# A gated scan layer re-cut into blocks of 1024 tokens, with one scan over two PSUM banks and the output projection six steps behind

## Chip, cores and metric

One core of a Trainium2 chip. The metric is the device time of one execution in microseconds (us), median of several runs. Engines are called as the profile calls them: PE (TensorE matmul), PEld (its weight loads), DVE (VectorE), ACT (ScalarE), POOL (GpSimd), SP (the queue that issues most transfers).

## The reference, cut to what matters

```
x: 8 sequences x 4224 tokens x 192      weight: 8 heads x 7 taps
w_in: 192 x 1024     A_log: 512     w_out: 512 x 192

x    = causal convolution of x along the tokens, softmax(weight) as taps, per head
proj = x @ w_in ;  val, gate = proj[..., :512], proj[..., 512:]
for t in range(S):                       # the scan, restarted in every sequence
    h = a * h + val[:, t] ;  ys[:, t] = h
out  = (silu(gate) * ys) @ w_out
```

The kernel computes in bf16 with fp32 sums and lays the 512 inner channels out as four groups (c = 0..3) of 128 partitions. All of its arithmetic is in SBUF and PSUM; the 33,792 tokens are walked in blocks.

## The kernel before

Blocks of 512 tokens, 66 of them. Per block: a convolution as matmuls against a banded matrix of taps (`tb`), eviction to bf16 (`xc`), then for each c a value projection (`pv`), a gate projection (`pg`), the scan on DVE, silu on ACT, the multiply `y`, and between them the output projection of the block before. Cut to what the argument touches:

```python
POOL_GATES = 2
    ps_c = ...tile_pool(name="ps_c", bufs=1, space=PSUM)     # pc: two banks
    ps_v = ...tile_pool(name="ps_v", bufs=2, space=PSUM)     # pv: one bank each
    ps_g = ...tile_pool(name="ps_g", bufs=2, space=PSUM)     # pg
    ps_o = ...tile_pool(name="ps_o", bufs=2, space=PSUM)     # po
    # ... taps: softmax, write 128 copies of the row to DRAM, read back shifted as tb ...
    # ... ab: decay table, 4 x 1024 fp32, built on DVE ...
    def cast(i, t):
        nc.gpsimd.tensor_copy(xbs[i % XB][:, :, 0:D], t)

    def scan(i, c, pv, prev):
        # ...
        nc.vector.tensor_tensor_scan(
            h, ab[:, c, a0 : a0 + N], pv,
            initial=prev[:, N - 1 : N] if prev is not None else 0.0,
            op0=Alu.mult, op1=Alu.add)

    def gate(i, c, pg, h):
        nc.scalar.activation(sg, pg, Act.Silu)
        eng = nc.gpsimd if c < POOL_GATES else nc.vector
        eng.tensor_mul(y, sg, h)

    for i in range(NS + 1):
        # load(i + 2); cast(i + 1)
        for c in range(NC):
            pv = proj(ps_v, "pv", xc, c)
            pg = proj(ps_g, "pg", xc, NC + c)
            hs[c] = scan(i, c, pv, hs[c])
            ys.append(gate(i, c, pg, hs[c]))
            outp(i - 1, ys_prev, c, ...)          # 4 matmuls, one per channel group
            # every second c: copy po to SBUF on ACT;  c == 1: conv(i + 1) and its eviction
        # store of block i - 1
```

## Time and profile before

| | before |
|---|---|
| time, median of three runs | 462.7 us (462.4 to 462.8) |
| profiled span | 460.6 us |
| busy: DVE / PE / ACT / POOL | 86% / 81% / 59% / 44% |
| period of 512 tokens | 6.43 us |
| first scan starts at | 31.5 us |

Busy shares are averages over the start, 66 like periods and the tail. The number that matters is the period, read from the starts of like instructions in order of time, and in it which wait ends last. The prediction shows these lines.

### The profile page before, as it was taken

What the parts mean: (1) busy time and instruction counts of PE and PEld (TensorE: products, weight loads), DVE (VectorE), ACT (ScalarE), POOL (GpSimd) and SP (SyncE); (2) the same over time, 40 slices, a digit from 0 to 9 for tenths busy, and PEclk for the clock granted to TensorE, in tenths of its full rate; (3) what the DMA queues carried; (4) which work ended last, traced back from release to release, by engine and by line L of the source; (5) the groups of instructions that cost most, each with busy time, mean ns of one, the idle gap of its engine ahead of it and who ended that gap; (6) DMA issues with size and microseconds to landing.
All of it is one profiled execution on the core that took longest, in us unless ns stands there. A gap on an engine that the chain in (4) does not pass through costs nothing.

```text
span 460.6 us, 11591 instructions
## 1 busy us (share of the span) xinstructions
PE 373.9 (81%) x4671; PEld 218.9 (48%) x4736; DVE 398.2 (86%) x415; ACT 271.9 (59%) x468; POOL 204.4 (44%) x205
## 2 busy tenths in 40 slices
PE   0048898888988898888988889888898888988884
PEld 0014555555554455554555545545454555555453
DVE  4259989999999999999999999999999999999995
ACT  1065666656665666656666566665666557665663
POOL 0114454445544455444554445544454445544442
PEclk9999999999999999999999999999999999999999
DMA  1901344433444334443444434444344433444323
GB/s 54 243 16 50 106 123 138 137 106 106 135 140 134 100 112 138 139 118 111 118 138 139 116 114 115 139 139 114 110 120 140 136 105 106 138 139 127 108 74 104
DMA packets 72469, 54.67 MB, mean 119 GB/s; under 512 B 4000, under 2 KB 72096, under 8 KB 72416
## 3 DMA queue, kind: packets, MB, share of 16 engines
q1 hardware_dynamic: 72128, 53.15, 40.1%
q10 hardware_dynamic: 288, 0.79, 0.7%
q8 instruction: 37, 0.61, 0.5%
q14 instruction: 16, 0.13, 0.1%
HBM read 27.44 MB, written 26.49 MB: 117 GB/s over the span
## 4 chain that ended last, share of the span: by engine, by line
DVE 51%; PE 38%; DMA 4%; issue 4%; ACT 1%; DVEq 1%; SPq 0%; ACTq 0%
DVE h L213 36%; PE pc L178 16%; DVE y L225 15%; PE po L230 9%; PE pv L203 7%; PE pg L203 7%; DMA wout<-in_moe_w_out_dram 2%; DMA win<-in_moe_w_in_dram 1%; DMA ws<-in_weight_dram 1%; DVEq L225 1%; DMA taps_scratch<-fz 1%; PE pc L187 1%; DVE fz L105 0%; SPq L130 0%; ACT xc L197 0%
## 5 line engine op out<-in xcount | busy, mean ns | idle before, releaser
L213 DVE TENSOR_TENSOR_SCAN h<-ab,h,pv 128x512 bf16<-128x512 f32 x260 | 324.5, 1269 | 22.4 <-PE pc L178 22.4
L225 POOL TENSOR_TENSOR y<-sg,h 128x512 bf16<-128x512 bf16 x132 | 152.5, 1155 | 226.2 <-DVE h L213 225.3
L222 ACT ACTIVATE sg<-pg 128x512 bf16<-128x512 f32 x264 | 157.6, 597 | 158.5 <-PE pg L203 158.5
L230 PE MATMUL po<-wout,y 128*128 128x192 bf16 x1056 | 141.3, 247 | 50.6 <-DVE y L225 50.6
L203 PE MATMUL pg<-xc,win 128*128 128x512 bf16 x528 | 157.7, 380 | 3.4
L230 PEld LDWEIGHTS <-y 128*128 128x128 bf16 x1056 | 95.9, 98 | 127.0 <-DVE y L225 65.6
L203 PE MATMUL pv<-xc,win 128*128 128x512 bf16 x463 | 144.6, 383 | 10.2 <-ACT xc L197 10.2
L203 PEld LDWEIGHTS <-win 128*128 128x128 bf16 x1056 | 95.3, 98 | 81.5 <-ACT win L150 8.7
L225 DVE TENSOR_TENSOR y<-sg,h 128x512 bf16<-128x512 bf16 x132 | 68.0, 515 | 14.2 <-DVE h L213 0.5
L197 ACT CAST xc<-pc 128x1024 bf16<-128x1024 f32 x66 | 66.8, 1012 | 0.1
L135 POOL CAST xb<-xraw 128x768 bf16<-128x768 f32 x66 | 54.6, 828 | 21.8 <-DMA xraw<-in_x_dram 19.9
L260 ACT COPY osb<-po 128x384 f32<-128x384 f32 x132 | 62.5, 474 | 2.1 <-issue 1.9
L178 PE MATMUL pc<-tb,xb 128*32 128x134 bf16 (+1 forms) x2112 | 46.6, 223 | 18.2 <-POOL xb L135 18.2
L178 PEld LDWEIGHTS <-xb 128*32 128x32 bf16 x2112 | 32.5, 95 | 28.8 <-POOL xb L135 18.2
L166 DVE TENSOR_SCALAR ab<-ab,av 128x1024 f32<-128x1024 f32 x4 | 2.7, 748 | 14.1 <-ACT av L162 14.1
L150 ACT CAST win<-win 128x2048 bf16<-128x2048 f32 x1 | 1.9, 1897 | 21.1 <-DMA win<-in_moe_w_in_dram 21.1
L187 PE MATMUL pc<-tb,xb 128*32 128x6 bf16 x512 | 13.1, 167 | 0.0
L187 PEld LDWEIGHTS <-xb 128*32 128x32 bf16 x512 | 10.6, 97 | 0.0
L213 DVE TENSOR_TENSOR_SCAN h<-ab,pv 128x512 bf16<-128x512 f32 x4 | 4.8, 1211 | 0.2
L164 DVE MEMSET ab<- 128x4096 f32 x1 | 3.5, 3472 | 0.8 <-issue 0.8
L95 DVE TENSOR_REDUCE wmax<-ws 128x8 f32<-128x56 f32 x1 | 0.2, 211 | 3.9 <-DMA ws<-in_weight_dram 3.9
L105 DVE MEMSET fz<- 128x2088 bf16 x1 | 1.8, 1798 | 0.4 <-issue 0.4
(16 smaller groups left out, 7.6 us busy)
## 6 DMA issues: line engine op xcount, KB each, us to landing
xraw<-in_x_dram SPq DMA_DIRECT2D x66, 384.0 KB, 3.9
out_dram<-osb SPq DMA_DIRECT2D x66, 384.0 KB
win<-in_moe_w_in_dram ACTq DMA_DIRECT2D x8, 96.0 KB
taps_scratch<-fz SPq DMA_DIRECT2D x1, 522.0 KB
wout<-in_moe_w_out_dram SPq DMA_DIRECT2D x1, 384.0 KB
tb<-taps_scratch SPq DMA_DIRECT2D x1, 268.0 KB
al<-in_moe_A_log_dram SPq DMA_DIRECT2D x4, 0.5 KB, 4.1
ws<-in_weight_dram SPq DMA_DIRECT2D x1, 28.0 KB
```

The costliest lines, as they stand in the source:

```text
L135: nc.gpsimd.tensor_copy(xbs[i % XB][:, :, 0:D], t)
L164: nc.vector.memset(ab, 1.0)
L166: nc.vector.tensor_scalar_mul(ab[:, c, :], ab[:, c, :], av[:, c : c + 1])
L178: nc.tensor.matmul(pc[q : q + 32, h // HG, b * P : b * P + w], xb[:, b, h * G : h * G + 32], tb[:, h, 0:w], start=(b == 0), stop=(b == NB ...
L187: nc.tensor.matmul(pc[q : q + 32, h // HG, 0:HALO], xp[:, NB - 1, h * G : h * G + 32], tb[:, h, P:W], start=False, stop=False, skip_group_ ...
L197: nc.scalar.copy(xc, pc)
L203: nc.tensor.matmul(ps, win[:, g, m * P : (m + 1) * P], xc[:, g, :], start=(g == 0), stop=(g == 1),)
L213: nc.vector.tensor_tensor_scan(h, ab[:, c, a0 : a0 + N], pv, initial=prev[:, N - 1 : N] if prev is not None else 0.0, op0=Alu.mult, op1=Al ...
L222: nc.scalar.activation(sg, pg, Act.Silu)
L225: eng.tensor_mul(y, sg, h)
L230: nc.tensor.matmul(po, ys[c][:, b * P : (b + 1) * P], wout[:, c, :], start=(c == 0 and b % 2 == 0), stop=(c == NC - 1), skip_group_check=True,
L260: nc.scalar.copy(osb[:, c - 1 : c + 1, :], po)
```

## The change

Intent: fewer and longer scans, less multiply work on DVE, no wait of PE for the last `y`, and a shorter start. Counted in banks, which here means places for a tile of up to 512 fp32 per partition, the kernel before takes eight of PSUM, two for each of its four pools. In the new one, two `pv` buffers of two banks and two banks for the convolution leave two of the same eight, which gate and output projection then share. The core of the diff:

```diff
-CAST = "pool"
-POOL_GATES = 2
+DVE_GATE = 1
+LAG = 6
...
-    ps_g = ctx.enter_context(tc.tile_pool(name="ps_g", bufs=2, space=bass.MemoryType.PSUM))
-    ps_o = ctx.enter_context(tc.tile_pool(name="ps_o", bufs=2, space=bass.MemoryType.PSUM))
+    ps_r = ctx.enter_context(tc.tile_pool(name="ps_r", bufs=2, space=bass.MemoryType.PSUM))
...
+    for h in range(H - 1):
+        nc.gpsimd.dma_start(                      # win straight to bf16, from POOL
+            win[C32 * (h % HG) : C32 * (h % HG) + C32, h // HG, :],
+            moe_w_in[h * G : h * G + C32, :],
+        )
...
-    nc.sync.dma_start(fa, fz.rearrange("p h f -> p (h f)"))
+    nc.scalar.dma_start(fa, fz.rearrange("p h f -> p (h f)"))
...
-            h, ab[:, c, a0 : a0 + N], pv,
+                h[:, lo:hi], av[:, c : c + 1].to_broadcast([P, hi - lo]), pv[:, lo:hi],
...
+    for s in range(NSTEP + LAG):                  # a step = one channel group of one block
+        i, c = divmod(s, NC)
+        if live:
+            # c == 0: load x three blocks ahead
+            scan(s)
+            if c == DVE_GATE + 1:
+                mul(nc.vector, s - 1)
+            gate(s, 0)
+        if s >= LAG:
+            outp(s - LAG)                         # 8 matmuls
+        if live:
+            if c % 2 == 0 and i + 1 < NS:
+                conv(2 * (i + 1) + c // 2)
+            val(s + 1, 0)
+            gate(s, 1)
+            val(s + 1, 1)
+            if c != DVE_GATE:
+                mul(nc.gpsimd, s)
+            else:
+                # cast x of two blocks ahead, on POOL
```

Also: six loads of x are issued at the start instead of two, the decay table is gone, and a block that holds the begin of a sequence gets its scan in two parts.

More of the change, by code (lines that the diff above doesn't have):

```diff
@@ L58 @@
     N = NB * P
+    N2 = 2 * N
     T = B * S
-    NS = T // N
+    NP = T // N
+    NS = T // N2
     BPB = S // P
@@ L63 @@
     HG = H // 2
-    assert NS * N == T and BPB * P == S and NC == 4 and G <= 32 and HG == 4
+    C32 = 32
+    assert NS * N2 == T and BPB * P == S and NC == 4 and G <= C32 and HG == 4
     W = P + HALO
-    XW = D + 8
     FL = P - 1
@@ L76 @@
     singles = ctx.enter_context(tc.tile_pool(name="singles", bufs=1))
-    xraw_pool = ctx.enter_context(tc.tile_pool(name="xraw", bufs=4))
-    xc_pool = ctx.enter_context(tc.tile_pool(name="xc", bufs=3))
+    xraw_pool = ctx.enter_context(tc.tile_pool(name="xraw", bufs=6))
+    xc_pool = ctx.enter_context(tc.tile_pool(name="xc", bufs=5))
     h_pool = ctx.enter_context(tc.tile_pool(name="hp", bufs=3))
@@ L84, with load @@
     ps_v = ctx.enter_context(tc.tile_pool(name="ps_v", bufs=2, space=bass.MemoryType.PSUM))
-    ps_g = ctx.enter_context(tc.tile_pool(name="ps_g", bufs=2, space=bass.MemoryType.PSUM))
-    ps_o = ctx.enter_context(tc.tile_pool(name="ps_o", bufs=2, space=bass.MemoryType.PSUM))
+    ps_r = ctx.enter_context(tc.tile_pool(name="ps_r", bufs=2, space=bass.MemoryType.PSUM))
+    XB = 4
+    raw = {}
+    def load(p):
+        t = xraw_pool.tile([P, NB, D], FP32, name="xraw")
+        nc.sync.dma_start(t, x4[p])
+        raw[p] = t
     FR = FL + W
@@ L93 @@
     )
+    load(0)
+    load(1)
+    win = singles.tile([P, 2, D2], BF16, name="win")
+    for h in range(H - 1):
[3 more added lines that the diff above has]
+        )
+    nc.gpsimd.dma_start(win[96 : 96 + G, 1, :], moe_w_in[(H - 1) * G : H * G, :])
+    nc.gpsimd.dma_start(win[96 + G : P, 1, :], moe_w_in[0 : C32 - G, :])
+    xbs = []
+    for j in range(XB):
+        xb = singles.tile([P, NB, H, C32], BF16, name=f"xb_{j}")
+        nc.gpsimd.memset(xb[:, :, :, G:C32], 0.0)
+        xbs.append(xb)
+    fz = singles.tile([P, H, FR], BF16, name="fz")
+    nc.vector.memset(fz, 0.0)
+    al = singles.tile([P, NC], FP32, name="al")
+    nc.scalar.dma_start(al, moe_A_log.rearrange("(c p) -> p c", p=P))
     wmax = singles.tile([P, H], FP32, name="wmax")
@@ L103 @@
     nc.vector.reciprocal(winv, wsum)
-    fz = singles.tile([P, H, FR], BF16, name="fz")
-    nc.vector.memset(fz, 0.0)
     for k in range(KW):
@@ L111 @@
     fa = f_dram.ap()
-    nc.sync.dma_start(fa, fz.rearrange("p h f -> p (h f)"))
+    nc.scalar.dma_start(fa, fz.rearrange("p h f -> p (h f)"))
     tb = singles.tile([P, H, W], BF16, name="tb")
-    nc.sync.dma_start(
+    nc.scalar.dma_start(
         tb, dataclasses.replace(fa, offset=FL, ap=[[H * FR - 1, P], [FR, H], [1, W]])
     )
-    XB = 3
-    xbs = []
-    for j in range(XB):
-        xb = singles.tile([P, NB, XW], BF16, name=f"xb_{j}")
-        nc.gpsimd.memset(xb[:, :, D:XW], 0.0)
-        xbs.append(xb)
@@ L125, in load @@
-    def load(i):
-        if CAST == "dma":
-            nc.gpsimd.dma_start(xbs[i % XB][:, :, 0:D], x4[i])
-            return None
-        t = xraw_pool.tile([P, NB, D], FP32, name="xraw")
-        nc.sync.dma_start(t, x4[i])
-        return t
-    def cast(i, t):
-        if CAST == "pool":
-            nc.gpsimd.tensor_copy(xbs[i % XB][:, :, 0:D], t)
-    raw = {}
-    for i in range(2):
-        raw[i] = load(i)
-    win32 = singles.tile([P, 2, D2], FP32, name="win32")
-    nc.vector.memset(win32, 0.0)
@@ L144 @@
-    for h in range(H):
-        nc.scalar.dma_start(
-            win32[32 * (h % HG) : 32 * (h % HG) + G, h // HG, :],
-            moe_w_in[h * G : (h + 1) * G, :],
-        )
-    win = singles.tile([P, 2, D2], BF16, name="win")
-    nc.scalar.copy(win, win32)
-    wout32 = singles.tile([P, NC, D], FP32, name="wout32")
-    nc.sync.dma_start(wout32, moe_w_out.rearrange("(c p) m -> p c m", p=P))
-    wout = singles.tile([P, NC, D], BF16, name="wout")
-    nc.scalar.copy(wout, wout32)
-    al = singles.tile([P, NC], FP32, name="al")
@@ L158, with cast @@
-    alog = moe_A_log.rearrange("(c p o) -> c p o", p=P, o=1)
-    for c in range(NC):
-        nc.sync.dma_start(al[:, c : c + 1], alog[c, :, :])
     av = singles.tile([P, NC], FP32, name="av")
     nc.scalar.activation(av, al, Act.Exp)
-    ab = singles.tile([P, NC, 2 * N], FP32, name="ab")
-    nc.vector.memset(ab, 1.0)
-    for c in range(NC):
-        nc.vector.tensor_scalar_mul(ab[:, c, :], ab[:, c, :], av[:, c : c + 1])
-    nc.vector.memset(ab[:, :, N : N + 1], 0.0)
-    def conv(i):
+    def cast(p):
+        nc.gpsimd.tensor_copy(
+            xbs[p % XB][:, :, :, 0:G],
+            raw.pop(p).rearrange("p b (h g) -> p b h g", g=G),
+        )
@@ L170, in conv @@
+    cast(0)
+    cast(1)
+    wout = singles.tile([P, NC, D], BF16, name="wout")
+    nc.gpsimd.dma_start(wout, moe_w_out.rearrange("(c p) m -> p c m", p=P))
+    for p in range(2, 6):
+        load(p)
+    cast(2)
+    cast(3)
+    xcs = {}
+    def conv(p):
         pc = ps_c.tile([P, 2, N], FP32, name="pc")
-        xb, xp = xbs[i % XB], xbs[(i - 1) % XB]
+        xb, xp = xbs[p % XB], xbs[(p - 1) % XB]
         for b in range(NB):
-            begins = (i * NB + b) % BPB == 0
-            ends = (i * NB + b + 1) % BPB == 0
+            begins = (p * NB + b) % BPB == 0
+            ends = (p * NB + b + 1) % BPB == 0
@@ L175, in conv @@
             w = P if ends or b == NB - 1 else W
             for h in range(H):
-                q = 32 * (h % HG)
+                q = C32 * (h % HG)
                 nc.tensor.matmul(
-                    pc[q : q + 32, h // HG, b * P : b * P + w],
-                    xb[:, b, h * G : h * G + 32],
+                    pc[q : q + C32, h // HG, b * P : b * P + w],
+                    xb[:, b, h, :],
                     tb[:, h, 0:w],
@@ L185, in conv @@
                 for h in range(H):
-                    q = 32 * (h % HG)
+                    q = C32 * (h % HG)
                     nc.tensor.matmul(
-                        pc[q : q + 32, h // HG, 0:HALO],
-                        xp[:, NB - 1, h * G : h * G + 32],
+                        pc[q : q + C32, h // HG, 0:HALO],
+                        xp[:, NB - 1, h, :],
                         tb[:, h, P:W],
@@ L192, in conv, with proj @@
                     )
-        return pc
-    def evac(pc):
         xc = xc_pool.tile([P, 2, N], BF16, name="xc")
         nc.scalar.copy(xc, pc)
-        return xc
-    def proj(pool, name, xc, m):
-        ps = pool.tile([P, N], FP32, name=name)
+        xcs[p] = xc
+    def proj(ps, p, m):
         for g in range(2):
             nc.tensor.matmul(
-                ps, win[:, g, m * P : (m + 1) * P], xc[:, g, :],
+                ps, win[:, g, m * P : (m + 1) * P], xcs[p][:, g, :],
                 start=(g == 0), stop=(g == 1),
@@ L206, in proj @@
             )
-        return ps
-    def scan(i, c, pv, prev):
-        cut = [b for b in range(NB) if (i * NB + b) % BPB == 0]
-        a0 = N - cut[0] * P if cut else 0
-        h = h_pool.tile([P, N], BF16, name=f"h_{c}")
-        nc.vector.tensor_tensor_scan(
-            h, ab[:, c, a0 : a0 + N], pv,
-            initial=prev[:, N - 1 : N] if prev is not None else 0.0,
-            op0=Alu.mult, op1=Alu.add,
-        )
-        return h
-    def gate(i, c, pg, h):
-        sg = g_pool.tile([P, N], BF16, name=f"sg_{c}")
-        nc.scalar.activation(sg, pg, Act.Silu)
-        y = y_pool.tile([P, N], BF16, name=f"y_{c}")
-        eng = nc.gpsimd if c < POOL_GATES else nc.vector
-        eng.tensor_mul(y, sg, h)
-        return y
@@ L228, in outp @@
-    def outp(i, ys, b, po):
-        for c in range(NC):
-            nc.tensor.matmul(
-                po, ys[c][:, b * P : (b + 1) * P], wout[:, c, :],
-                start=(c == 0 and b % 2 == 0), stop=(c == NC - 1), skip_group_check=True,
-            )
-    cast(0, raw.pop(0))
-    xc = evac(conv(0))
-    hs = [None] * NC
-    ys_prev = None
-    for i in range(NS + 1):
-        if i < NS:
-            if i + 2 < NS:
-                raw[i + 2] = load(i + 2)
-            if i + 1 < NS:
-                cast(i + 1, raw.pop(i + 1))
-        ys = []
-        xc_next = None
-        if ys_prev is not None:
-            osb = o_pool.tile([P, NB, D], FP32, name="osb")
-        for c in range(NC):
-            if i < NS:
-                pv = proj(ps_v, "pv", xc, c)
-                pg = proj(ps_g, "pg", xc, NC + c)
-                hs[c] = scan(i, c, pv, hs[c])
-                ys.append(gate(i, c, pg, hs[c]))
-            if ys_prev is not None:
-                if c % 2 == 0:
-                    po = ps_o.tile([P, 2, D], FP32, name="po")
-                outp(i - 1, ys_prev, c, po[:, c % 2, :])
-                if c % 2 == 1:
-                    nc.scalar.copy(osb[:, c - 1 : c + 1, :], po)
-            if c == 1 and i + 1 < NS:
-                xc_next = evac(conv(i + 1))
-        if ys_prev is not None:
-            nc.sync.dma_start(o4[i - 1], osb)
-        ys_prev = ys
-        xc = xc_next
@@ new lines, with val, gate @@
+    pvs = {}
+    def val(s, half):
+        i, c = divmod(s, NC)
+        if i >= NS:
+            return
+        if half == 0:
+            pvs[s] = ps_v.tile([P, N2], FP32, name="pv")
+        proj(pvs[s][:, half * N : (half + 1) * N], 2 * i + half, c)
+    sgs = {}
+    def gate(s, half):
+        i, c = divmod(s, NC)
+        if half == 0:
+            sgs[s] = g_pool.tile([P, N2], BF16, name=f"sg_{c}")
+        pg = ps_r.tile([P, N], FP32, name="pr")
+        proj(pg, 2 * i + half, NC + c)
+        nc.scalar.activation(sgs[s][:, half * N : (half + 1) * N], pg, Act.Silu)
@@ new lines, with scan @@
+    last = [None] * NC
+    hs = {}
+    def scan(s):
+        i, c = divmod(s, NC)
+        h = h_pool.tile([P, N2], BF16, name=f"h_{c}")
+        pv = pvs.pop(s)
+        cuts = [b * P for b in range(2 * NB) if (i * 2 * NB + b) % BPB == 0]
+        ends = sorted(set([0] + cuts + [N2]))
+        for lo, hi in zip(ends, ends[1:]):
+            nc.vector.tensor_tensor_scan(
+                h[:, lo:hi], av[:, c : c + 1].to_broadcast([P, hi - lo]), pv[:, lo:hi],
+                initial=0.0 if lo in cuts else last[c],
+                op0=Alu.mult, op1=Alu.add,
+            )
+            last[c] = h[:, hi - 1 : hi]
+        hs[s] = h
@@ new lines, with mul, outp @@
+    ys = {}
+    def mul(eng, s):
+        y = y_pool.tile([P, N2], BF16, name=f"y_{s % NC}")
+        eng.tensor_mul(y, sgs.pop(s), hs.pop(s))
+        ys[s] = y
+    osbs = {}
+    def outp(v):
+        i, u = divmod(v, NC)
+        p = 2 * i + u // 2
+        po = ps_r.tile([P, N], FP32, name="pr")
+        po2 = po[:, 0 : 2 * D].rearrange("p (b d) -> p b d", d=D)
+        for k in range(2):
+            t0 = (2 * u + k) * P
+            for c in range(NC):
+                nc.tensor.matmul(
+                    po2[:, k, :], ys[NC * i + c][:, t0 : t0 + P], wout[:, c, :],
+                    start=(k == 0 and c == 0), stop=(c == NC - 1), skip_group_check=True,
+                )
+        if u % 2 == 0:
+            osbs[p] = o_pool.tile([P, NB, D], FP32, name="osb")
+        b0 = 2 * (u % 2)
+        nc.scalar.copy(osbs[p][:, b0 : b0 + 2, :], po2)
+        if u % 2 == 1:
+            nc.sync.dma_start(o4[p], osbs.pop(p))
@@ new lines @@
+    NSTEP = NS * NC
+    conv(0)
+    conv(1)
+    val(0, 0)
+    val(0, 1)
+    for s in range(NSTEP + LAG):
+        i, c = divmod(s, NC)
+        live = s < NSTEP
+        if live:
+            if c == 0:
+                for p in (2 * (i + 3), 2 * (i + 3) + 1):
+                    if p < NP:
+                        load(p)
+            scan(s)
[13 more added lines that the diff above has]
+            else:
+                for p in (2 * (i + 2), 2 * (i + 2) + 1):
+                    if p < NP:
+                        cast(p)
```

## The prediction

> **What bounds the kernel now.** I read the page's busy line and its chain first, then the groups by shape, then the order of time over one period, then the first 32 us. Busy shares:
>
> ```profile
> PE 373.9 (81%) x4671; PEld 218.9 (48%) x4736; DVE 398.2 (86%) x415; ACT 271.9 (59%) x468; POOL 204.4 (44%) x205
> ```
>
> VectorE (DVE) leads, but an average over start, steady state and tail does not say whether it alone is the limit. The chain that ended last:
>
> ```profile
> DVE 51%; PE 38%; DMA 4%; issue 4%; ACT 1%; DVEq 1%; SPq 0%; ACTq 0%
> ```
>
> It goes back and forth between DVE and TensorE (PE): a loop in which each waits for the other once per period. The groups by shape give the costs (count, then busy us and mean ns of one):
>
> ```profile
> L213 DVE TENSOR_TENSOR_SCAN h<-ab,h,pv 128x512 bf16<-128x512 f32 x260 | 324.5, 1269 | 22.4 <-PE pc L178 22.4
> L222 ACT ACTIVATE sg<-pg 128x512 bf16<-128x512 f32 x264 | 157.6, 597 | 158.5 <-PE pg L203 158.5
> L225 POOL TENSOR_TENSOR y<-sg,h 128x512 bf16<-128x512 bf16 x132 | 152.5, 1155 | 226.2 <-DVE h L213 225.3
> L230 PE MATMUL po<-wout,y 128*128 128x192 bf16 x1056 | 141.3, 247 | 50.6 <-DVE y L225 50.6
> L225 DVE TENSOR_TENSOR y<-sg,h 128x512 bf16<-128x512 bf16 x132 | 68.0, 515 | 14.2 <-DVE h L213 0.5
> L197 ACT CAST xc<-pc 128x1024 bf16<-128x1024 f32 x66 | 66.8, 1012 | 0.1
> L135 POOL CAST xb<-xraw 128x768 bf16<-128x768 f32 x66 | 54.6, 828 | 21.8 <-DMA xraw<-in_x_dram 19.9
> L260 ACT COPY osb<-po 128x384 f32<-128x384 f32 x132 | 62.5, 474 | 2.1 <-issue 1.9
> ```
>
> One period of 512 tokens, in order of time (start us, us):
>
> ```profile
> 205.19 2.45 DVE L213 TENSOR_TENSOR_SCAN h<-ab,h,pv 128x512 bf16<-128x512 f32 x2
> ...
> 205.42 0.59 PE L203 MATMUL pv<-xc,win 128*128 128x512 bf16 x2
> 205.86 0.59 PE L203 MATMUL pg<-xc,win 128*128 128x512 bf16 x2
> ...
> 208.22 0.49 PE L230 MATMUL po<-wout,y 128*128 128x192 bf16 x4
> ...
> 208.55 0.59 PE L203 MATMUL pv<-xc,win 128*128 128x512 bf16 x2
> ...
> 210.61 0.41 PE L230 MATMUL po<-wout,y 128*128 128x192 bf16 x3
> ...
> 211.76 0.26 PE L230 MATMUL po<-wout,y 128*128 128x192 bf16 x1 [0.74 <-DVE y L225]
> 211.85 0.59 PE L203 MATMUL pv<-xc,win 128*128 128x512 bf16 x2
> ```
>
> Starts count here, since matmuls overlap. From pv at 205.42 to pv at 211.85 is one period: 6.43 us; 66 of them are 424 of the 460.6 us. Of it PE needs 210.61 - 205.42 = 5.19 us for all but the last po group, plus 0.33 for that group (208.22 to 208.55), 5.52 in all. The remaining 0.91 is the wait of the fourth po matmul for y on DVE. DVE is busy about 5.9 us of 6.43 (58.8 of 64.3 in three windows of ten periods). So DVE sets the pace, helped by two short waits, and PE stands only 0.9 us beneath it. That decides what the change is worth.
>
> The start is the other 30 us:
>
> ```profile
> 18.15 1.07 PE L178 MATMUL pc<-tb,xb 128*32 128x134 bf16 x32 [18.15 <-POOL xb L135]
> ...
> 25.73 1.90 ACT L150 CAST win<-win 128x2048 bf16<-128x2048 f32 x1 [21.05 <-DMA win<-in_moe_w_in_dram]
> ...
> 31.48 3.66 DVE L213 TENSOR_TENSOR_SCAN h<-ab,pv 128x512 bf16<-128x512 f32 x3
> ```
>
> Convolution at 18, the weights only at 25.7, the first scan at 31.5 because the decay table is built after them.
>
> [...]
>
> **The change, part by part, per block of 1024 tokens.** (a) *Scan of 1024 over two banks:* [...] Sequences of 4224 tokens begin inside seven blocks, so 28 scans are cut in two[...]. [...] (b) *Gate multiplies:* POOL takes three channel groups of four instead of two. DVE's share falls from four multiplies of 512 (4 x 0.515 = 2.06) to one of 1024[...]. (c) *POOL:* with no fixed part known, twice 1155 ns, 2.3 us, for 1024; three and two casts of 0.83 make 8.6 us. The cast writes runs of 24 elements now; even at double cost POOL has 10.2. (d) *ACT is unchanged:* 8 x 0.597 + 2 x 1.01 + 4 x 0.474 = 8.7 us. (e) *PE is unchanged:* the same matmuls, 2 x 5.52 = 11.04 us. It is now the longest.
>
> So the limit moves from DVE to PE[...]: 12.86 - 11.04 = 1.8 us, 33 blocks, 60 us. (f) *Lag of six steps:* outp of a block starts two steps after the last gate multiply of that block was released, and that multiply takes 2.3 us against steps of 2.4 to 3.1; the 0.9 us wait for y goes. (g) *Gate and out-proj share two banks:* each use must wait until ACT has drained the use before last. I worked one pair of steps through by hand. A step with convolution on PE: gate half 0 (0 to 0.435), out-proj (to 1.10), convolution with its switch (to 1.83), val, gate half 1 (2.26 to 2.70), val (to 3.13). ACT, 0.2 us behind: silu to 1.24, copy to 1.77, eviction 2.02 to 3.03, second silu to about 3.6. The out-proj of the next step wants that bank at 3.57 and gets it at 3.6 to 3.7: a stall of about 0.06 to 0.12. The step without convolution has none. Two a block, 0.06 each: 4 us. (h) *val's two buffers of two banks:* val(s+1) needs scan(s-1) finished, which ends more than 1 us before it is asked for.
>
> **The sum.** PE work: 66 x 5.52 = 364, plus 4 of bank stalls. Start: the decay table, two casts of weights and 1.8 us of clearing go; the taps come about 2 us earlier. But the weights now come by nine casting DMAs that POOL issues ahead of the first cast of x, six loads of x are issued at once, and two convolutions, with one PSUM buffer between them (an eviction of 1.0 between), must precede the first scan. About 4.3 MB is to land, and the fastest slice of the page moved 243 GB/s: 18 us until all is in, the taps before that. I put the first convolution at 15.5 and the first scan at 20.3 us (an estimate, 17 to 25). 2.2 us of PE's 364 are done by then. [...] Table load for silu: +1. Tail: the last POOL multiply, 2.1 us that PE waits for, then copy and store, 4.4 (3.7 from the last copy to the end now). Span: 20.3 + 362 + 4 + 2 + 1 + 2.1 + 4.4 = 396. The timed median lies 2.1 above the profiled span (462.7 against 460.6): **398 us**, 14% less.
>
> **Rivals.** *DVE stays the bound[...].* If its multiply meets a POOL multiply of 2.3 us and waits it out, [...]. For: both are released near the end of the same scan, and the means 515 against 426 show that blocking exists. Against: POOL's multiply also waits for the second silu, at 3.6 in its step by the working above, when the DVE multiply[...] is over; only a cast can be in its way. *The shared banks throttle PE.* If ACT falls behind by a whole silu in each step (0.3 of stall), 33 x 4 x 0.3 = 40 us come back: 434. For: ACT has 8.7 of 11 us in strict order, with an eviction ahead of a silu. Against: the step without convolution gives ACT time to catch up. *The scan gains nothing from length*[...], so the time hardly moves. *The start takes longer* because POOL is slow to issue casting DMAs: the trace has no DMA issued by POOL, so I have no duration for one; each microsecond is one of the total, up to 410.
>
> **Range and chances.** The floor is 364 of PE work with a start of 16 and a tail of 6: about 388 with the timed offset. The top allows a late start (+5) and a few tenths of stall in each block (+9): 412. [...] faster 0.97, same 0.02, slower 0.01.
>
> **What would show it.** PE's pv-to-pv pattern with hardly a wait: period 11.0 to 11.3 us per 1024, PE at 92% or more of the span after the start; the chain mostly PE; [...]. Wrong would be: scans much over 2.4; DVE multiplies of 2 us or more[...]; PE idle before out-proj or gate, released by ACT (banks); a first scan after 25 us.

The sum came to 396 us of span, and 398 timed with the 2.1; of its seven terms, the 2 for the first six steps is one that is cut, and without it 394 and 396 are left. The 1 for the silu table stands for a load of 1.28 us in the trace before (at 29.39 us).

That the limit moves to PE can be had from the trace before alone, as an estimate: two scans of 512 in a row took 2.45 us (at 205.19) and a DVE multiply of 512 has a median of 426 ns, so four scans and one multiply of twice that length need 4 x 2.45 + 2 x 0.426 = 10.65 us per block if length saves nothing and no scan is cut, under PE's 11.04. The same trace shows what the first rival is about: beside a cast on POOL (208.88 to 209.70) a DVE multiply took 0.60 us (at 209.38), with none beside it 0.42 (at 211.28).

## The result, and the profile after

| | before | after |
|---|---|---|
| time, median | 462.75 us (462.44 to 463.80) | 399.53 us (399.16 to 400.88) |
| ratio | | 0.8636 (95%: 0.8611 to 0.8660) |
| profiled span | 460.6 us | 397.6 us |
| busy: DVE / PE / ACT / POOL | 86 / 81 / 59 / 44% | 84 / 92 / 72 / 68% |
| period per 1024 tokens | 12.86 us | 11.02 us |
| first convolution, first scan at | 18.2, 31.5 us | 23.3, 28.9 us |

Ratios are the mean time of one kernel's fast runs over that of the other's fast runs of the same rounds, so not quite the ratio of the medians in the table.

The busy line and the chain of the kernel after:

```profile
PE 366.6 (92%) x4736; PEld 222.6 (56%) x4736; DVE 332.3 (84%) x205; ACT 287.0 (72%) x466; POOL 268.6 (68%) x183
PE 89%; DMA 5%; DVE 2%; ACT 1%; issue 1%; DVEq 1%; POOLq 1%; ACTq 0%
```

The chain no longer goes back and forth: it is PE from the start to the end. DVE fell by only two points in share (332 of 398 us against 398 of 461), which shows how little a share says about which engine sets the pace. The groups by shape (count, then busy us and mean ns; then idle time before them and who ended it):

```profile
L233 DVE TENSOR_TENSOR_SCAN h<-av,h,pv 128x1024 bf16<-128x1024 f32 x100 | 234.3, 2345 | 23.9 <-PE pv L198 20.7 <-PE pr L198 0.4
L245 POOL TENSOR_TENSOR y<-sg,h 128x1024 bf16<-128x1024 bf16 x99 | 210.9, 2131 | 115.0 <-ACT sg L221 109.6 <-DVE y L245 3.4 <-DVE h L233 1.5
L258 PE MATMUL pr<-wout,y 128*128 128x192 bf16 x1056 | 108.3, 246 | 1.7 <-POOL y L245 1.7
L245 DVE TENSOR_TENSOR y<-sg,h 128x1024 bf16<-128x1024 bf16 x33 | 22.0, 666 | 0.0
```

The out-proj's wait for `y` is 1.7 us in the whole kernel, once, at the very end; it was 50.6. Scans now wait for PE. The DVE multiply takes 665 to 668 ns in all 33 places: it is never lengthened. One block in order of time (start us, us):

```profile
203.21 0.30 PE L177 MATMUL pc<-tb,xb 128*32 128x134 bf16 x8
...
207.66 1.60 POOL L152 CAST xb<-xraw 128x768 bf16<-128x768 f32 x2
...
208.72 0.30 PE L177 MATMUL pc<-tb,xb 128*32 128x134 bf16 x8
...
210.10 0.67 DVE L245 TENSOR_TENSOR y<-sg,h 128x1024 bf16<-128x1024 bf16 x1
...
211.11 2.12 POOL L245 TENSOR_TENSOR y<-sg,h 128x1024 bf16<-128x1024 bf16 x1 [1.85 <-ACT sg L221]
...
214.23 0.30 PE L177 MATMUL pc<-tb,xb 128*32 128x134 bf16 x8
```

From one first convolution of a block to the next is 11.02 us, with no wait on PE in between. The casts end at 209.26, 0.84 us before the DVE multiply starts, and the POOL multiply begins 0.34 us after it has ended. The start, in order of time:

```profile
1.19 16.85 SPq L94 DMA_DIRECT2D xraw<-in_x_dram  x10
...
8.05 0.35 ACTq L141 DMA_DIRECT2D taps_scratch<-fz  x1
...
15.12 0.38 ACTq L143 DMA_DIRECT2D tb<-taps_scratch  x1
...
23.33 1.07 PE L177 MATMUL pc<-tb,xb 128*32 128x134 bf16 x32 [23.33 <-DMA tb<-taps_scratch]
```

The taps leave DVE at 8.05, where they left it before too, but are written by 15.1 (10.8 before), and the convolution waits for them until 23.3.

### The profile page after: what moved, and what is told of

Same layout as the page of the kernel before. It is cut to its first block, busy times and chain, and to the rows that moved or that the text cites. A ratio compares the mean times of both kernels' runs of the same rounds, so it can differ in the third digit from the quotient of the medians.

```text
span 397.6 us, 11114 instructions
## 1 busy us (share of the span) xinstructions
PE 366.6 (92%) x4736; PEld 222.6 (56%) x4736; DVE 332.3 (84%) x205; ACT 287.0 (72%) x466; POOL 268.6 (68%) x183
## 4 chain that ended last, share of the span: by engine, by line
PE 89%; DMA 5%; DVE 2%; ACT 1%; issue 1%; DVEq 1%; POOLq 1%; ACTq 0%
PE pv L198 30%; PE pr L198 28%; PE pr L258 21%; PE pc L177 10%; DMA tb<-taps_scratch 2%; DMA taps_scratch<-fz 2%; DMA ws<-in_weight_dram 1%; DVE h L233 1%; ACT xc L193 1%; DVEq L325 1%; PE pc L186 1%; POOLq L325 1%; DVE y L245 0%; DVE fz L136 0%; ACT sg L221 0%
## 5 line engine op out<-in xcount | busy, mean ns | idle before, releaser
L233 DVE TENSOR_TENSOR_SCAN h<-av,h,pv 128x1024 bf16<-128x1024 f32 (+7 forms) x128 | 270.1, 2112 | 30.3 <-PE pv L198 26.5
L245 POOL TENSOR_TENSOR y<-sg,h 128x1024 bf16<-128x1024 bf16 x99 | 210.9, 2131 | 115.0 <-ACT sg L221 109.6
L221 ACT ACTIVATE sg<-pr 128x512 bf16<-128x512 f32 x264 | 157.7, 597 | 67.0 <-PE pr L198 67.0
L198 PE MATMUL pv<-xc,win 128*128 128x512 bf16 x528 | 158.5, 382 | 0.8 <-DVE h L233 0.6
L198 PE MATMUL pr<-xc,win 128*128 128x512 bf16 x528 | 157.3, 380 | 0.1
L258 PE MATMUL pr<-wout,y 128*128 128x192 bf16 x1056 | 108.3, 246 | 1.7 <-POOL y L245 1.7
L258 PEld LDWEIGHTS <-y 128*128 128x128 bf16 x1056 | 91.0, 98 | 32.2 <-POOL y L245 1.9
L177 PE MATMUL pc<-tb,xb 128*32 128x134 bf16 (+1 forms) x2112 | 47.0, 225 | 24.4 <-DMA tb<-taps_scratch 23.3
L265 ACT COPY osb<-pr 128x384 f32<-128x384 f32 x132 | 63.3, 479 | 8.3 <-PE pr L258 2.9
L233 DVE TENSOR_TENSOR_SCAN h<-av,pv 128x1024 bf16<-128x1024 f32 (+7 forms) x32 | 42.5, 1330 | 21.2 <-PE pv L198 21.2
L245 DVE TENSOR_TENSOR y<-sg,h 128x1024 bf16<-128x1024 bf16 x33 | 22.0, 666 | 0.0
```

What stands on the lines that cost most here:

```text
L177: nc.tensor.matmul(pc[q : q + C32, h // HG, b * P : b * P + w], xb[:, b, h, :], tb[:, h, 0:w], start=(b == 0), stop=(b == NB - 1), skip_gr ...
L198: nc.tensor.matmul(ps, win[:, g, m * P : (m + 1) * P], xcs[p][:, g, :], start=(g == 0), stop=(g == 1),)
L221: nc.scalar.activation(sgs[s][:, half * N : (half + 1) * N], pg, Act.Silu)
L233: nc.vector.tensor_tensor_scan(h[:, lo:hi], av[:, c : c + 1].to_broadcast([P, hi - lo]), pv[:, lo:hi], initial=0.0 if lo in cuts else last[c],
L245: eng.tensor_mul(y, sgs.pop(s), hs.pop(s))
L258: nc.tensor.matmul(po2[:, k, :], ys[NC * i + c][:, t0 : t0 + P], wout[:, c, :], start=(k == 0 and c == 0), stop=(c == NC - 1), skip_group_ ...
```

## The experiments

Twelve kernels, each timed against the kernel before on its own chip. The theory to be tested: PE sets the pace at 11.02 us per block, and a change of any other engine's work counts only for what exceeds it. The first rival: DVE still sets it.

**1. The long scan undone.**

```diff
-        ends = sorted(set([0] + cuts + [N2]))
+        ends = sorted(set([0, N] + cuts + [N2]))
```

> The changed kernel with each scan of 1024 cut into two of 512 (the long scan undone, all else kept). In the changed kernel's trace a cut scan takes 1.28 + 1.19 = 2.47 us against 2.35, so DVE gets about 0.12 x 4 = 0.5 us more per block of 1024, 10.0 to 10.5, still under PE's period of 11.02. Theory (PE sets the pace): time as the changed kernel, 399.5 within 2 us. Rival (DVE at 84% still sets the pace and PE only looks full): 33 x 0.5 = 16 us more, about 416.

Measured: 401.75 us, ratio 0.8698 (0.8678 to 0.8719). 2.2 us more than the changed kernel: just beyond the 2 us that I had allowed, and far from 16. The two traces place it: the first copy of an output comes 1.4 us later (45.0 against 43.6; the first six steps have no out-proj, and PE waits for scans there, 0.26 and 0.35 us in the changed kernel; such waits come to 1.5 us in this run) and the last 2.3 us later (395.9 against 393.6). Of the remaining 0.9, 0.8 is a longer wait for the last `y` (2.5 against 1.7). In the steady state the long scan is worth nothing here. The rival falls.

**2 and 3. Two, then three gate multiplies on DVE.**

```diff
-DVE_GATE = 1
+DVE_GATES = (1, 3)          # run 3: (1, 2, 3)
...
-            if c == DVE_GATE + 1:
+            if s > 0 and (s - 1) % NC in DVE_GATES:
                 mul(nc.vector, s - 1)
...
+        if s == NSTEP and (s - 1) % NC in DVE_GATES:
+            mul(nc.vector, s - 1)
...
-            if c != DVE_GATE:
+            if c not in DVE_GATES:
                 mul(nc.gpsimd, s)
-            else:
+            if c == 1:
```

> The changed kernel with two gate multiplies of four on DVE instead of one, POOL two instead of three. DVE gets 0.67 us more per block, 10.0 to 10.7, under PE's 11.02. Theory (PE sets the pace): 399.5 within 3 us. Rival (DVE sets the pace): 33 x 0.67 = 22 us more, about 421.

> The changed kernel with three gate multiplies of four on DVE. DVE gets 1.33 us more per block, 10.0 to 11.35, which passes PE's 11.02. Theory: the limit changes over to DVE here, and only the excess of 0.33 us per block counts: 33 x 0.33 = 11 us more, about 410 (up to 415 with hand-over gaps). Rival (DVE sets the pace already): 33 x 1.33 = 44 us more, about 443.

Measured: 398.69 us, ratio 0.8622 (0.8604 to 0.8641), and 399.43 us, ratio 0.8641 (0.8626 to 0.8657). Two are as expected. Three should have cost 11 us and cost nothing: I had added durations, and neighbours on DVE overlap. The order of time on DVE in the run with three:

```profile
214.16 2.34 DVE L233 TENSOR_TENSOR_SCAN h<-av,h,pv 128x1024 bf16<-128x1024 f32 x1
216.42 0.67 DVE L245 TENSOR_TENSOR y<-sg,h 128x1024 bf16<-128x1024 bf16 x1
217.00 4.58 DVE L233 TENSOR_TENSOR_SCAN h<-av,h,pv 128x1024 bf16<-128x1024 f32 x2
```

From start to start a scan before a multiply holds DVE 2.26 us, a multiply 0.58, a scan before a scan 2.24 (4.58 - 2.34). So three multiplies make 3 x 2.84 + 2.24 = 10.8 us per block, about 10.9 with the cut scans, still under 11.02.

**4. All four on DVE**, where these starts say that DVE should pass PE. The same edit with `(0, 1, 2, 3)`.

> The changed kernel with all four gate multiplies on DVE. By starts (not durations) in the run with three, a scan holds DVE 2.26 us and a multiply 0.58, so DVE needs 4 x 2.84 = 11.4 us per block and 0.1 for cut scans, against PE's 11.02. Theory: here DVE becomes the limit and only the excess counts: 33 x 0.4 to 0.5 = 13 to 16 us more, 412 to 416, a little more if multiplies meet casts on POOL. Rival (DVE's work is hidden whatever it is): 399.

Measured: 414.86 us, ratio 0.8969 (0.8955 to 0.8982), 15.3 us more than the changed kernel, as the excess of about 0.45 us in 33 blocks says. DVE is busy in 222.0 of 222 us of the steady state. The change-over lies between three and four multiplies.

**5. Less work for PE.** Its output is wrong, which doesn't matter for the time.

```diff
-            for c in range(NC):
+            for c in range(NC - 1):
                 nc.tensor.matmul(po2[:, k, :], ...
-                    start=(k == 0 and c == 0), stop=(c == NC - 1), ...
+                    start=(k == 0 and c == 0), stop=(c == NC - 2), ...
```

> The changed kernel without one of the four matmuls of each out-proj sum (a wrong result on purpose). PE loses 8 matmuls of 0.083 us per block, 0.66 us: 11.02 to 10.36, still over DVE's 10.0. Theory (PE sets the pace): 33 x 0.66 = 22 us less, about 378. Rival (DVE sets the pace): no change, 399.

Measured: 377.75 us, ratio 0.8164 (0.8142 to 0.8186): 21.8 us less, as expected. Taking work from PE counts in full; giving DVE up to 0.9 us more (run 3) counts nothing. PE is the bound.

**6. A lag of four steps.**

```diff
-LAG = 6
+LAG = 4
```

> The changed kernel with the out-proj four steps behind instead of six. The last POOL multiply of a block starts about 2.9 us into its step (after the second silu), takes 2.12, and so ends about 2.6 us into the next step of PE; with a lag of four the out-proj asks for it 0.44 us into that step. Theory: PE waits about 2.1 us once per block, 32 times: 60 to 70 us more, about 465, with a wait of the out-proj for POOL's y of that size in the trace. Rival (the lag is only worth the 0.9 us wait per 512 tokens that the kernel before showed, or ACT's and POOL's order moves up by itself): at most 30 us more, below 430.

Measured: 471.47 us, ratio 1.0208 (1.0178 to 1.0238), at a mean granted clock of 0.984 in the profiled run: no gain over the kernel before, and a loss of about 2%. In order of time:

```profile
207.91 2.12 POOL L245 TENSOR_TENSOR y<-sg,h 128x1024 bf16<-128x1024 bf16 x1 [0.26 <-ACT sg L221]
...
210.08 0.59 PE L258 MATMUL pr<-wout,y 128*128 128x192 bf16 x5 [1.77 <-POOL y L245]
```

PE stands 1.77 us and continues 0.05 us after POOL's multiply; the block takes 12.96 us from out-proj to out-proj (200.01 to 212.97). 33 x 1.94 makes 64 of the 72 us. Most of the other 8 goes with the clock, by an estimate: 468.5 us of span at a mean granted clock of 0.984 are 468.5 x 0.016 = 7.5 us more than at 1.0. Why the clock was lower is not shown. From 100 to 322 us the granted clock is 1.00, and there, with a lag of four, a block takes 12.96 us against 12.86 in the kernel before, so the new order is no gain at all. A lag of five was not run.

The run does not decide between the theory and the rival as I wrote it. The kernel before waits 0.91 us per 512 tokens, so 1.8 us per 1024, which is the wait found here. My 30 us for the rival is 33 x 0.9, which counts the wait once per 1024 tokens instead of twice.

**7. The kernel before, with three gate multiplies on POOL.**

```diff
-POOL_GATES = 2
+POOL_GATES = 3
```

> The kernel before with one number changed: three gate multiplies of four on POOL instead of two. DVE loses about 0.5 us per 512 tokens, 5.9 to 5.4, POOL has 3 x 1.155 + 0.83 = 4.3, PE 5.52. Theory (gate balance is most of the gain, the long scan is not needed): a period of 5.6 to 5.8 instead of 6.43, about 410 to 420 us. Rival (the gain needs the new order, because PE and DVE wait for each other through the val buffers and the last y): above 440.

Measured: 458.56 us, ratio 0.9927 (0.9907 to 0.9947). My theory fell: 0.7% instead of 10%. The trace says where it went, and it is not where the rival put it. One period's DVE multiply and its neighbours, in order of time:

```profile
202.09 0.82 POOL L135 CAST xb<-xraw 128x768 bf16<-128x768 f32 x1
...
202.12 1.07 DVE L225 TENSOR_TENSOR y<-sg,h 128x512 bf16<-128x512 bf16 x1
...
203.25 0.26 PE L230 MATMUL po<-wout,y 128*128 128x192 bf16 x1 [0.72 <-DVE y L225]
```

With a third multiply on POOL, its cast of x moved to 0.03 us before the one multiply that DVE keeps, and that one took 0.64 us longer (median 1067 ns against 426), with PE behind it. This is the collision of the prediction's first rival, with a cast in the place of POOL's multiply, met in another kernel. The kernel before already met this once per period (its two DVE multiplies take 0.60 and 0.42 us, the first beside a cast). So two multiplies of 1.02 us together became one of 1.07, and DVE saved nothing.

**8. The same, with the cast on ACT**, so that no cast runs on POOL beside the DVE multiply.

```diff
-            nc.gpsimd.tensor_copy(xbs[i % XB][:, :, 0:D], t)
+            nc.scalar.copy(xbs[i % XB][:, :, 0:D], t)
```

> The kernel before with three gate multiplies on POOL, as in the run that came to 458.6, and the cast of x moved from POOL to ACT, so that POOL has no cast when the remaining DVE multiply starts. In that run the DVE multiply rose to a median of 1067 ns because it began 0.03 us after a cast. Theory[...]: the DVE multiply is back at about 0.43, the period 6.4 - 0.64 = 5.8 us, the time about 416 (412 to 425). Rival (val buffers of one bank and the last y make PE and DVE wait for each other whatever the multiply takes): the multiply is short and the time still above 445.

Measured: 420.88 us, ratio 0.9111 (0.9091 to 0.9131). DVE in order of time over a period:

```profile
199.93 0.42 DVE L225 TENSOR_TENSOR y<-sg,h 128x512 bf16<-128x512 bf16 x1
...
205.69 0.42 DVE L225 TENSOR_TENSOR y<-sg,h 128x512 bf16<-128x512 bf16 x1
```

The multiply is back at 0.42 us (median of all 425 ns) and the period is 5.76 us. The longer multiply beside the cast had taken back 37.7 us (458.56 to 420.88). The edit also takes the casts off POOL, but POOL was busy in only 280.0 of 456.7 us in run 7, so its load was not the limit there. Two edits of the old kernel, with blocks of 512, thus reach two thirds of the change's gain (41 of 63 us). What the new order adds from there: 5.76 to 5.51 us per 512 tokens, 16.5 us, mostly PE's last waits for `y` (the last out-proj group holds PE 0.58 us from start to start, 199.92 to 200.50, the others 0.33); a first scan at 28.9 instead of 32.3, 3.4 us; 1.5 us are not placed.

**9. The decay as a table again.**

```diff
+    ab = singles.tile([P, NC, N2], FP32, name="ab")     # filled with av on DVE
...
-                h[:, lo:hi], av[:, c : c + 1].to_broadcast([P, hi - lo]), pv[:, lo:hi],
+                h[:, lo:hi], ab[:, c, lo:hi], pv[:, lo:hi],
```

> The changed kernel with the decay read from a full table in SBUF instead of one element at stride zero. Theory: the stride makes no difference to the scan (mean of a 1024 scan 2.35 us in both) and the table is built while the start waits for the taps, so 399.5 within 2 us. Rival (stride zero is what makes scans shorter): scans of 1024 above 2.4 us; hidden under PE in the steady state, but seen in their mean.

Measured: 399.64 us, ratio 0.8650 (0.8633 to 0.8667); a scan of 1024 has a mean of 2345 ns in both kernels. The stride makes no difference, and the table is built while the taps are waited for (first scan at 28.65 us, 28.88 in the changed kernel).

**10 to 12. The start.** The first scan came 8.6 us later than I had predicted, and the wait is for the taps. Two suspects are under way at the same time: ten loads of x, issued from 1.19 to 18.04 us, and the nine casting transfers of the weights, issued from 1.26 to 9.83.

Run 10, taps on the queue that loads x, ahead of its third load:

```diff
-    nc.scalar.dma_start(fa, fz.rearrange("p h f -> p (h f)"))
+    nc.sync.dma_start(fa, fz.rearrange("p h f -> p (h f)"))
...
-    nc.scalar.dma_start(
+    nc.sync.dma_start(
         tb, ...
```

> The changed kernel with the two tap transfers issued on the queue that loads x, ahead of the third load, so that only two loads of x compete with them. Theory (the loads of x issued ahead of need slow the taps: the write to scratch takes 7.0 us and the read back 8.2, against 2.7 and about 4.5 in the kernel before): first convolution at about 15.5 to 17 us instead of 23.3, and the time 6 to 8 us less, about 392. Rival (the weights' casting transfers from POOL, or the transfers themselves, take that time): less than 2 us gained.

Run 11, only the weights later:

```diff
-    for h in range(H - 1):
-        nc.gpsimd.dma_start(win[...], ...)        # and two more, ahead of everything on POOL
...
     cast(0)
     cast(1)
+    for h in range(H - 1):
+        nc.gpsimd.dma_start(win[...], ...)        # and two more
```

> The changed kernel with the nine casting transfers of the input weights issued after the first two casts of x instead of first. Theory (the loads of x slow the taps more than the weights do): first convolution one to two us earlier than 23.3, about 22, and the time 397 to 398.5 unless the weights then come after the first convolution and are waited for. Rival (the weights slow the taps): first convolution at 19 or earlier.

Run 12, both, and the last multiply of all on DVE:

```diff
-                mul(nc.gpsimd, s)
+                mul(nc.vector if s == NSTEP - 1 else nc.gpsimd, s)
```

> A version to beat both: taps ahead of the third load of x (394.6 alone), the weights' casting transfers after the first two casts, and the very last gate multiply on DVE, which is idle then, instead of POOL. Theory: only the two first loads of x share with the write to scratch, so it takes about 3 to 4 us instead of 6.4: first convolution at 14.5 to 15.5, 2.5 to 3.5 us earlier; the tail 1.6 us shorter; time about 389 to 391. Rival: the weights land too late and the first projection waits for them, 393 or more.

| | taps written in | read back in | first convolution | time | ratio |
|---|---|---|---|---|---|
| changed kernel | 7.0 us | 8.2 us | 23.33 | 399.53 | 0.8636 |
| 10, taps first | 6.4 | 4.0 | 17.89 | 394.62 | 0.8548 (0.8525 to 0.8571) |
| 11, weights late | 6.2 | 7.1 | 20.78 | 397.67 | 0.8598 (0.8581 to 0.8615) |
| 12, both | 2.8 | 3.5 | 13.23 | 391.18 | 0.8463 (0.8447 to 0.8479) |

The second and third columns are from issue to landing. With all but two loads of x behind the taps in one queue, the reading back takes 4.0 us instead of 8.2. (Run 10 also moves the taps from ACT's queue to SP's; the queue alone was not tested.) The write stays slow as long as either suspect is there, 6.2 to 6.4, and takes 2.8 only without both: each of my single causes was half right. Run 10 missed its expectation (17.89 us and 394.62, where 15.5 to 17 and about 392 were expected), and run 11's convolution came between its theory and its rival. Of the 10.1 us by which run 12 brings the first convolution forward, 4.2 are the write, 4.7 the reading back and 1.1 an earlier issue of the write (6.94 instead of 8.05). In run 12 the rival came true in part:

```profile
13.23 1.07 PE L177 MATMUL pc<-tb,xb 128*32 128x134 bf16 x32 [13.23 <-DMA tb<-taps_scratch]
...
19.13 1.46 PE L198 MATMUL pv<-xc,win 128*128 128x512 bf16 x3 [2.04 <-DMA win<-in_moe_w_in_dram]
```

The weights now arrive 2.04 us after PE wants them, so the earlier taps are not used in full; the time is still under the rival's 393. The tail did what it should: PE's last wait for `y` is 0.23 us (1.70 before the edit). Run 12 is correct and beats both kernels, by 15.4% and by 2%.

## Why the prediction was right

It said 398 us; 399.53 was measured, inside the range. The mechanism held: the limit moved to PE. That the sum came within 1.5 us is luck, because the start was 8.6 us too short and other terms were too long by nearly as much. So the steps deserve a closer look.

- *The limit moves from DVE to PE at 11.04 us per block:* shown. 11.02 measured; work off PE counts in full (run 5), work onto DVE counts from the point where it passes PE (runs 2 to 4).
- *The costs of 1024 tokens:* measured, a scan takes 2.24 to 2.26 from start to start; the DVE multiply is 0.67 long, 0.58 from start to start. *POOL's multiply at 2.3:* 2.12. *Casts not slower for runs of 24 elements:* 0.83 and, two in a row, 0.80. DVE needs per block, by the starts of run 3, three scans at 2.24, one at 2.26 and one multiply at 0.58, which make 9.6, and the cut scans bring it to about 9.7.
- *The lag removes the wait for y:* shown by run 6. The size is the one in the trace before: a lag of four waits 1.77 us per block of 1024, the kernel before 0.91 us per 512.
- *Two shared banks cost 4 us:* the trace after has no wait of PE for ACT in the steady state, so this term was about 0. The opposite, gate and output projection in banks of their own beside the two-bank scan, would need ten, two more than either kernel takes, and was not run; that the sharing is free rests on the trace alone.
- *The start:* the term that failed. First convolution 15.5 predicted, 23.33 measured; first scan 20.3 and 28.88, so 8.6 us, beyond my stated 17 to 25, and a first scan after 25 us was one of the signs of being wrong that I had named. I took the total of bytes over the fastest slice's rate and assumed that the taps would land ahead of the rest. I also counted six loads of x, and the trace has ten issued by 18.04 us. The taps are the longest chain (two transfers, one after the other) and were slowed by transfers that nobody was waiting for yet (runs 10 to 12).
- *What offset it:* from the first scan to PE's last matmul 371.1 us were predicted (362 + 4 + 2 + 1 + 2.1) and 364.7 measured (28.88 to 393.56). The shared banks give 4 of the difference. The silu table load, which I put there as 1 us, ran from 27.73 to 29.01, nearly all of it ahead of the first scan. The last wait for `y` was 1.7 instead of 2.1. Of the remaining 1 us, 0.7 is the shorter period (33 x 0.02); the rest is not placed. The tail after PE was 4.0 instead of 4.4.
- *The first rival, DVE's multiply held up by POOL:* it did not come true in this kernel (the multiply took 665 to 668 ns everywhere), and for the reason given, the order of events: casts end 0.84 us before, POOL's multiply starts 0.34 us after. Runs 7 and 8 show that the danger was real: a DVE multiply that starts 0.03 us after a cast takes 1067 ns instead of 425, and in the old order with three multiplies on POOL that costs 38 us.
- *What I would not have guessed:* the words of the change name the long scan, the stride-zero decay and the shared banks. The first two are worth nothing in the steady state (runs 1 and 9), and the last makes room for the first. Nor does POOL's third multiply count alone: with two or three multiplies on DVE the time is the same (runs 2 and 3). Of the parts that were taken back one at a time, only the lag costs the gain (run 6). That does not make the relief of DVE needless. Without the long scan and with two multiplies on DVE at once, DVE would come to about 11.1 us per block (212.4 of 222 us busy in run 1, so 10.54, and 0.58 more), an estimate, just over PE's 11.02. And the lag alone in the old order could bring its period of 6.43 us down to DVE's 5.9 at most, 35 of the 63 us, an estimate too. Neither was run.

## What to carry to other kernels

When two engines need nearly the same time per block (here 12.86 us with DVE in the lead, and PE's 11.04), work taken from the first counts only down to the second: find the second one's period from the starts of its instructions, not from durations, which overlap (a scan of 2.34 us held DVE 2.26). Moving work to another engine also moves *when* its instructions run, and an instruction that then starts beside another one's can take so much longer that the whole gain is given back (run 7: 1067 ns instead of 426 for a DVE multiply beside a POOL cast); look at the duration of the instruction that did not move. At the start, issue what the longest chain needs first and hold back prefetch until it has landed (first convolution at 13.23 us in run 12, 23.33 in the changed kernel).

## What the traces show of single instructions

- The scan: the eight lengths in the trace after, from 128 to 1024 elements, give 2.10 ns per element (396 to 2278 ns, a constant as the initial value), on top of about 0.13 us. An initial value that is read from the `h` tile before adds 0.07 to 0.09 us (479 against 396 ns at 128, 2345 against 2278 at 1024). Two banks in one scan change nothing (1194 ns at 512, 2278 at 1024, both on that line), nor does a decay at stride zero (2345 ns with it and with the table).
- The bf16 multiply on POOL: 1155 ns at 512 elements and 2124 at 1024 (medians), a slope of (2124 - 1155) / 512 = 1.89 ns per element.
- The price of prefetch at the start: the same 522 KB write took 2.8 us with two loads of x issued ahead of it (run 12) and 6.2 to 7.0 with more loads of x, the casting transfers of the weights, or both.
